# A recurrent attention block and an MLP in one kernel: loads of 48 rows instead of 128, four copies on another engine, and new orders of the work

## The chip, the cores and the metric

The kernel runs on one core of a Trainium2 chip. The metric is the device time of one execution in microseconds. The kernel before was run nine times: the median is 659.54 us, the lowest 658.38, the highest 661.29.

## The reference

For each of 4 batches and 8 heads, a state of 48 x 48 numbers is updated at each of 768 time steps and read out; the result goes through an MLP (384 to 2048 to 384) with a PReLU between. All of it is in float32.

```python
f = 1.0 / (1.0 + np.exp(-f_logit))
state = np.zeros((B, H, D, D))                 # B 4, H 8, D 48
for t in range(S):                             # S 768
    state = f[:, :, t, :, None] * state + np.einsum('bhd,bhe->bhde', k[:, :, t], v[:, :, t])
    y[:, :, t] = np.einsum('bhd,bhde->bhe', q[:, :, t], state)
x = y.transpose(0, 2, 1, 3).reshape(B * S, H * D)      # 3072 tokens of 384
h = x @ w_in                                   # 384 x 2048
g = np.maximum(h, 0.0) + alpha * np.minimum(h, 0.0)
out = g @ w_out                                # 2048 x 384
```

## The kernel before

**Steps.** Time is cut into 6 chunks of 128 and the batches into 2 pairs, so there are 12 steps (a chunk of a batch pair, 256 tokens); the chunk is the outer loop. Inside a chunk the recurrence is done without a loop over time: products of decays are formed for runs of 4 and blocks of 32 time steps, and matmuls build a matrix A of decayed products of q and k, which is then multiplied with v and, through the same matmuls, with the state carried from the half chunk before. The state lies in spare rows of the tile `vs`, beside v.

**Layout.** A head has 48 dimensions. Even heads lie in partitions 0 to 47, odd heads in 64 to 111 (`rows(par)`). The arrays `qT`, `kT`, `fT` in memory have 128 rows for each chunk, of which rows 48 to 63 and 112 to 127 are zeros put there by the host (`by_dim`). A load in `prepare` brings all 128 rows of a batch pair: 512 KB.

**Stages.** Each step has four Python generators. Each `next` on one of them emits one piece.

- `prepare` (6 pieces): loads of f, q, k and v; ScalarE takes the sigmoid of f (L250) and copies (L251, L253); VectorE multiplies decays into `qd` (L258 to L266). Then running sums of decays by VectorE, four copies into `us` by ScalarE (L275); the products `us` (L280, L289), `k4` (L295), `q3`, `ks`, `kh` (L307 to L328) on VectorE; last four copies of q3 into A by ScalarE (L340).
- `carry` (2 pieces): matmuls `off` (L356) with copies into A (L361) and transposes `pk` (L369) with copies into `ksn` (L372); then matmuls `pd` (L381) and `moved(0)`, which brings the state a half chunk on: VectorE multiplies the old state (L391) and adds the increment `pd` (L395). Where there is no state yet (chunk 0, first half) the increment is only copied (L397).
- `attend` (6 pieces): for each batch u of the pair, matmuls `raw` (L416) and `qu` (L431), whose results VectorE writes into `ad` under masks (L422, L436); two pieces of copies from ad into A by ScalarE (L445), one for each u; matmuls `py` (L456); then `moved(1)`, two copies of py into y (L465) and eight heads' DMAs that bring y in the layout `xT` (L472, half of them issued by ScalarE, half by SP).
- `network` (12 pieces): eight pieces, each of 6 matmuls `ph` (L486; two records each in the profile, 12 in all), a Relu by ScalarE (L491, `neg`) and two operations of VectorE that give `g` (L494); then matmuls `po` (L502) in four quarters, the last with the copies (L508) and the DMAs of the output.

**Weights.** `load_weights` gives two pairs of generators: `a` and `w` for w_in, `b` and `v` for w_out, 12 pieces each. An upper piece (`a`, `b`) is a DMA by SP (L163) and two operations of ScalarE (L168, L170). A rest piece (`w`, `v`) is three operations of VectorE (`lead` L176, `rest` L188, `power` L182: a triple) and a DMA of GpSimd that adds the leading parts to the tile (L191).

**Buffers.** PSUM tiles of the attention stages are `pair`s, of which there are two: raw, qu, raw, qu, off, pk, pd and py take turns. ph and po share four banks. The tiles f, q and k of a step come from the pool `work` with one buffer each.

**Order.** TensorE, VectorE and ScalarE execute exactly in the order in which the program emits; the queues of GpSimd and SP are ordered by a scheduler. The order comes from strings. In turn n, `P`, `O` and `S` stand for a piece of prepare, carry and attend of step n, `n` for a piece of the network of step n-1, `Q` for a piece of prepare of step n+1; a number repeats a key, and a key with nothing left is skipped. Turns 0 to 3 have their own strings (`first`), the other turns use `usual`. Turn n=2 so runs step 2's attention with step 1's network, and the fourth entry (n=3) step 3's attention with step 2's network.

```python
    def begin(n):
        ...
        return [stage(*steps[n], x) for stage in (prepare, carry, attend, network)]
...
            on = pieces | {"P": prep, "O": car, "S": att, "z": filling, "n": before, "Q": coming}
            for key in (first[n] if n < len(first) else usual).split():
                for _ in range(int(key[1:] or 1)):
                    if on[key[0]] is not None:
                        next(on[key[0]])
```

Of the kernel before, what the change touches and what calls it, by code (L numbers as in the profile page):

```python
# [8 lines left out]
F32 = mybir.dt.float32  # L9
# [12 lines left out]
U = 2  # L22
# [8 lines left out]
def kernel(  # L31
# [28 lines left out]
    nc = tc.nc  # L60
    B, NC, _, HP, _ = qT.shape
    DM = v.shape[-1]
    H = 2 * HP
# [5 lines left out]
    W = U * HP * C  # L69
# [12 lines left out]
    const = ctx.enter_context(tc.tile_pool(name="const", bufs=1))  # L82
    work = ctx.enter_context(tc.tile_pool(name="work", bufs=2))
# [3 lines left out]
    def pair(name):  # L87
        return psa.tile([128, 2, 512], F32, tag="pair", name=name)
# [35 lines left out]
    for m in range(1, NB):  # L124
        lo = UO[m] + (4 if m == 1 else 0)
        n = NB - m
# [4 lines left out]


    A = const.tile([128, U, H, C], F32, tag="A", name="A")
    nc.gpsimd.memset(A, 0.0)
    vs = []
    for bp in range(B // U):
# [75 lines left out]
    def rows(par):  # L212
        return slice(64 * par, 64 * par + D)

    def quads(t):
        return t.rearrange("p (n r) -> p n r", r=4)

    def halves(cc):

        return slice(CH * cc, CH * cc + CH), slice(CH * (1 - cc), CH * (1 - cc) + D)  # L220
# [8 lines left out]
    def prepare(bp, c, x):  # L229

        i = f"{bp}_{c}"
        b0 = U * bp
        loads = nc.gpsimd if bp or c else nc.sync

        def load(name, src, bufs=2):
            t = work.tile([128, W], F32, tag=name, name=f"{name}_{i}", bufs=bufs)
            loads.dma_start(out=t.rearrange("p (u x) -> p u x", u=U),  # L237
                              in_=src[b0:b0 + U, c].rearrange("u p h t -> p u (h t)"))
            return t

        f = quads(load("f", fT, 1))
        q = load("q", qT, 1)
        k = x["k"] = load("k", kT, 1)

        for cc in range(NC2):
            t_, _ = halves(cc)
# [25 lines left out]
        us = x["us"] = work.tile([128, G, UW], F32, tag="us", name=f"us_{i}", bufs=1)  # L272
# [21 lines left out]
        k4 = x["k4"] = work.tile([128, W], F32, tag="k4", name=f"k4_{i}", bufs=1)  # L294
# [43 lines left out]
        for cc in range(NC2):  # L338
            for par in range(2):
                nc.scalar.copy(A[halves(cc)[1], :, par * HP:(par + 1) * HP, CH * cc:CH * (cc + 1)],  # L340
                               q3[rows(par)].rearrange("p (u h c) s t -> p u h c (s t)", h=HP, c=NC2)[:, :, :, cc, 0:CH])
        yield

    def carry(bp, c, x):

        i = f"{bp}_{c}"
        q3, ks, kh, f64 = (x[n] for n in ("q3", "ks", "kh", "f64"))
        off = pair(f"off_{i}")
        for u in range(U):
            for hp in range(HP):  # L350
                for cc in range(NC2):
                    g = (u * HP + hp) * NC2 + cc
                    o = (u * HP + hp) * DB
                    for par in range(2):
                        r_ = rows(par)
                        nc.tensor.matmul(off[CH * cc:CH * cc + DB, par, o:o + DB],  # L356
                                         lhsT=kh[r_, g], rhs=q3[r_, g, 2], start=True, stop=True)
        for cc in range(NC2):
            s_ = slice(CH * cc, CH * cc + DB)
            for par in range(2):  # L360
                nc.scalar.copy(A[s_, :, par * HP:(par + 1) * HP, CH * cc + DB:CH * (cc + 1)],  # L361
                               off[s_, par, 0:U * HP * DB].rearrange("p (u h t) -> p u h t", u=U, h=HP))


        pk = pair(f"pk_{i}")
        for u in range(U):
            for hp in range(HP):
                a = (u * HP + hp) * NC2
                nc.tensor.transpose(pk[:, u, hp * 128:(hp + 1) * 128], ks[:, a:a + 2].rearrange("p c s t -> p (c s t)"), ident)  # L369
        ksn = work.tile([128, U, HP * 128], F32, tag="ksn", name=f"ksn_{i}", bufs=1)  # L370
        for u in range(U):
            nc.scalar.copy(ksn[:, u], pk[:, u])  # L372
        yield
        pd = pair(f"pd_{i}")
        for u in range(U):
            for hp in range(HP):
                for cc in range(NC2):
                    for par in range(2):
                        o = (u * HP + hp) * D
                        s_ = halves(cc)[0]  # L380
                        nc.tensor.matmul(pd[64 * par:64 * par + 64, cc, o:o + D],  # L381
                                         lhsT=ksn[s_, u, hp * 128 + 64 * par:hp * 128 + 64 * par + 64],
                                         rhs=vs[bp][s_, cc, u, (2 * hp + par) * D:(2 * hp + par + 1) * D], start=True, stop=True)

        def moved(cc):

            of, to = halves(cc)[1], halves(1 - cc)[1]
            was, then = (vs[bp][p, a, :, 0:DM].rearrange("p u (h e) -> p u h e", e=D)
                         for p, a in ((of, cc), (to, 1 - cc)))
            if c or cc:  # L390
                nc.vector.tensor_tensor(then, was, f64[of].unsqueeze(3).broadcast_to((D, U, H, D)), ALU.mult)  # L391
            for par in range(2):
                now = pd[rows(par), cc, 0:U * HP * D].rearrange("p (u h e) -> p u h e", u=U, e=D)
                if c or cc:
                    nc.vector.tensor_tensor(then[:, :, par:H:2], then[:, :, par:H:2], now, ALU.add)  # L395
                else:
                    nc.vector.tensor_copy(then[:, :, par:H:2], now)  # L397

        x["moved"] = moved
        moved(0)  # L400
        yield

    def attend(bp, c, x):

        i = f"{bp}_{c}"
        k, k4, us = (x[n] for n in ("k", "k4", "us"))


        for u in range(U):
            raw = pair(f"raw{u}_{i}")  # L410
            for hp in range(HP):
                for j in range(NJ):
                    g = (u * HP + hp) * NJ + j
                    for par in range(2):
                        r_ = rows(par)
# [4 lines left out]
            for d in range(4):  # L420
                n = 4 - d
# [4 lines left out]
            for hp in range(HP):  # L426
                for j in range(NJ):
                    g = (u * HP + hp) * NJ + j
                    for par in range(2):
                        r_ = rows(par)  # L430
                        nc.tensor.matmul(qu[DB * j:DB * (j + 1), par, hp * UW + 4:(hp + 1) * UW],  # L431
                                         lhsT=k4[r_, g * DB:(g + 1) * DB], rhs=us[r_, g, 4:UW], start=True, stop=True)
            for m in range(1, NB):
                lo = UO[m] + (4 if m == 1 else 0)
                n = DB - 4 * m
# [6 lines left out]
        for u in range(U):  # L442
            for j in range(NJ):
                s_ = slice(DB * j, DB * (j + 1))
                nc.scalar.copy(A[s_, u, :, s_], ad[s_, u].rearrange("p r h t -> p (r h) t"))  # L445
            yield
# [3 lines left out]
        for u in range(U):  # L450
            for hp in range(HP):
                for cc in range(NC2):
                    for par in range(2):
# [3 lines left out]
                                         lhsT=vs[bp][:, cc, u, hd * D:hd * D + 64],  # L457
                                         rhs=A[:, u, par * HP + hp, CH * cc:CH * (cc + 1)],
                                         start=True, stop=True)
# [7 lines left out]
        for hd in range(H):  # L467
            d = hd * D
            while d < (hd + 1) * D:
                n = min((hd + 1) * D, (d // 128 + 1) * 128) - d  # L470
                p0 = 64 * (hd % 2) + d - hd * D
                (nc.sync if hd % 2 else nc.scalar).dma_start(  # L472
                    out=xT[d % 128:d % 128 + n, d // 128].rearrange("p (u t) -> p u t", u=U),
                    in_=y[p0:p0 + n, :, hd // 2])
# [3 lines left out]
    def network(bp, c, x):  # L478
# [37 lines left out]

    steps = [(bp, c) for c in range(NC) for bp in range(B // U)]
    first = (
        "P2 a2 P2 w a2 w P O w P a w S2 O w Q S2 a w a S a S Q w2",
        "a P w a w a P w n P a n w b v w S b v n b n O v b v n b v S P S n b O b v n b S v2 n2 S n b v Q b v b n v b v2 Q3 S n Q",  # L520
        "n2 O n S n2 S Q S n S O n2 Q n Q2 n P S n S Q n Q",
        "n S n2 S Q n2 O n S n S Q n O Q2 n Q S2 Q n3",
    )
    usual = "O n2 S n2 S2 n O n Q n Q n S n2 S Q n S Q2 n Q"
    pieces = {key: part for keys, parts in (("aw", load_weights(w_in_sb, w_in, "w_in")),
                                            ("bv", load_weights(w_out_sb, w_out, "w_out")))
              for key, part in zip(keys, parts)}
# [1 line left out]
    def begin(n):  # L529
        if n >= len(steps):  # L530
            return [None] * 4
        x = {}
        return [stage(*steps[n], x) for stage in (prepare, carry, attend, network)]
# [68 lines left out]
```

## Time and profile before

The profiled execution took 659.54 us itself; its span, from the first to the last instruction, is 657.7 us. In the first 110 us the weights come in beside the first steps.

| what | value | from |
| --- | --- | --- |
| time, nine runs | 659.54 us median, 658.38 to 661.29 | times |
| profiled execution, span | 659.54 us, 657.7 us | profile |
| read from and written to HBM | 36.21 MB, 4.72 MB | page, part 3 |
| instructions of ph and po | 265.2 and 252.7 us of TensorE | page, part 5 |
| loads of f, q, k by GpSimd | 11 each, 512 KB, 4.3, 4.2, 4.5 us to landing | page, part 6 |
| loads of v by GpSimd | 22, 192 KB, 3.5 us to landing | page, part 6 |
| first off of step 0 | 18.45 us | timeline |
| first ph of steps 0 and 1 | 48.03 and 109.08 us | timeline |
| last weight DMA landed | 106.13 us | timeline |
| off of steps 4 and 5 | 210.2 and 260.6 us | timeline |

How to read it: an instruction that waits holds up all later ones of its engine. The list of waits gives, for each kind, how long the engine stood idle in total, how often, and the longest. A timeline row gives start, length and engine of a run of like instructions, and in brackets the idle time before it with what ended it. Granted clock 0.50 means that TensorE's matmuls take twice as long. A matmul in float32 shows as several instructions, so the counts are multiples of the calls in the code.

### The profile page before, as it was taken

The page shows a single profiled execution, that of the slowest core. Times are in us where ns is not written, and L with a number is a line of the kernel's source. Part 1 is how long each engine was busy: PE and PEld are TensorE (multiplying, and loading weights), DVE is VectorE, ACT ScalarE, POOL GpSimd, SP SyncE. Part 2 cuts the span into 40 slices and gives each one's busy share as a digit, 9 for nine tenths or more (in the row PEclk, how much of TensorE's full clock was granted, in tenths as well). Part 3 has the DMA queues.
Part 4 walks back from the last instruction along what each step waited for, and adds up shares of the span by engine and source line. Part 5 has one row for each costly group of instructions (what it writes and reads, how often), then busy time and mean ns, then how long its engine had stood idle before and what let it go on. Part 6 is the DMA issues. An engine that isn't in the chain of part 4 may idle for free.

```text
span 657.7 us, 17032 instructions
## 1 busy us (share of the span) xinstructions
PE 616.7 (94%) x7392; PEld 458.8 (70%) x7392; DVE 420.3 (64%) x897; ACT 266.8 (41%) x493; POOL 68.8 (10%) x109
## 2 busy tenths in 40 slices
PE   0547999999999999999999999999999999999997
PEld 0435866866876876876876876876876786786874
DVE  5999889693873685685585586486387486360220
ACT  5854892543443242451451550550460451430210
POOL 7222332000010000000000001001001000000000
PEclk9967999999999999999999999999999999999999
DMA  7979986122212113113113023023023011001000
GB/s 223 321 194 267 268 250 158 39 62 73 66 38 69 34 56 83 34 34 92 29 51 81 29 64 81 26 66 80 26 66 81 26 34 25 26 2 25 24 1 24
DMA packets 29129, 53.03 MB, mean 81 GB/s; under 512 B 4320, under 2 KB 16864, under 8 KB 29056
## 3 DMA queue, kind: packets, MB, share of 16 engines
q0 software_dynamic: 9616, 27.92, 15.8%
q1 hardware_dynamic: 13584, 21.63, 10.7%
q10 hardware_dynamic: 5856, 2.40, 1.7%
q8 instruction: 58, 0.95, 0.6%
q14 instruction: 15, 0.12, 0.1%
HBM read 36.21 MB, written 4.72 MB: 62 GB/s over the span
## 4 chain that ended last, share of the span: by engine, by line
PE 90%; DVE 5%; ACT 1%; POOL 1%; issue 1%; ACTq 1%; DVEq 0%; POOLq 0%
PE ph L486 38%; PE po L502 38%; PE py L456 3%; PE qu L431 3%; PE raw L416 3%; PE pd L381 2%; PE pk L369 2%; PE off L356 1%; DVE us L289 1%; DVE ad L436 1%; ACTq L472 1%; POOL vs L138 0%; DVE w_in_lead L176 0%; DVE us L280 0%; ACT w_in_pos L168 0%
## 5 line engine op out<-in xcount | busy, mean ns | idle before, releaser
L486 PE MATMUL ph<-xT,w_in_sb 128*128 128x256 f32 x1152 | 265.2, 387 | 8.8 <-DMA xT<-y 8.7
L502 PE MATMUL po<-w_out_sb,g 128*128 128x384 f32 x768 | 252.7, 488 | 0.0
L486 PEld LDWEIGHTS ph<-xT,w_in_sb 128*128 128x128 f32 x1152 | 218.3, 193 | 43.9 <-DMA w_in_sb<-w_in_lead 8.5
L502 PEld LDWEIGHTS po<-w_out_sb,g 128*128 128x128 f32 x768 | 144.8, 190 | 97.1 <-DMA w_out_sb<-w_out_lead 0.4
L494 DVE SCALAR_TENSOR_TENSOR g<-neg,om,ph 128x256 f32<-128x256 f32 x192 | 83.3, 477 | 151.8 <-ACT neg L491 151.6
L491 ACT ACTIVATE neg<-ph 128x512 f32<-128x512 f32 x96 | 57.7, 601 | 153.2 <-PE ph L486 125.0
L508 ACT COPY o<-po 128x384 f32<-128x384 f32 x24 | 11.5, 479 | 114.3 <-PE po L502 106.4
L436 DVE COPY_PREDICATED ad<-mquad,qu 128x224 f32<-128x224 int32 (+6 forms) x168 | 50.4, 300 | 8.4 <-DVE ad L422 0.5
L465 ACT COPY y<-py 128x512 f32<-128x512 f32 x24 | 12.9, 588 | 81.1 <-PE py L456 81.1
L289 DVE TENSOR_TENSOR us<-us,fs 128x768 f32<-128x768 f32 (+2 forms) x72 | 44.6, 620 | 0.3
L422 DVE COPY_PREDICATED ad<-mraw,raw 128x256 f32<-128x256 int32 (+1 forms) x96 | 42.4, 442 | 2.7
L445 ACT COPY A<-ad 32x256 f32<-32x256 f32 x96 | 38.4, 400 | 3.8 <-DVE ad L436 2.5
L391 DVE TENSOR_TENSOR vs<-vs,f 48x768 f32<-48x768 f32 x20 | 19.0, 952 | 30.4 <-PE py L456 30.0
L275 ACT COPY us<-qd 128x256 f32<-128x256 f32 x48 | 29.6, 664 | 12.2 <-DVE qd L258 7.6
L431 PE MATMUL qu<-us,k 48*32 48x112 f32 x1536 | 27.7, 276 | 5.1 <-DVE us L289 3.4
L258 DVE TENSOR_TENSOR qd<-qd,f 128x768 f32<-128x768 f32 (+2 forms) x36 | 27.4, 760 | 8.0 <-ACT qd L253 8.0
L340 ACT COPY A<-q 48x512 f32<-48x512 f32 x48 | 29.6, 617 | 6.2 <-DMA xT<-y 5.5
L237 POOL DMA_DIRECT2D k<-in_kT x11 | 8.4, 761 | 221.7 <-PE raw L416 196.7
L456 PEld LDWEIGHTS py<-A,vs 128*64 128x64 f32 x768 | 25.1, 145 | 7.2 <-issue 6.5
L456 PE MATMUL py<-A,vs 128*64 128x64 f32 x768 | 26.9, 231 | 0.9 <-DVE vs L397 0.5
L356 PE MATMUL off<-q,kh 48*32 48x32 f32 x768 | 9.4, 199 | 18.5 <-DVE q L307 18.5
L431 PEld LDWEIGHTS qu<-us,k 48*32 48x32 f32 x1536 | 22.1, 111 | 5.7 <-ACT w_out_pos L168 3.6
(64 smaller groups left out, 447.3 us busy)
## 6 DMA issues: line engine op xcount, KB each, us to landing
w_in_raw<-in_w_in SPq DMA_DIRECT2D x12, 511.8 KB, 5.6
w_out_raw<-in_w_out SPq DMA_DIRECT2D x12, 511.8 KB, 5.2
f<-in_fT POOLq DMA_DIRECT2D x11, 512.0 KB, 4.3
q<-in_qT POOLq DMA_DIRECT2D x11, 512.0 KB, 4.2
k<-in_kT POOLq DMA_DIRECT2D x11, 512.0 KB, 4.5
out<-o SPq DMA_DIRECT2D x24, 192.0 KB, 1.9
vs<-in_v POOLq DMA_DIRECT2D x22, 192.0 KB, 3.5
w_in_sb<-w_in_lead POOLq DMA_DIRECT2D x12, 256.0 KB, 5.7
```

Source lines behind the costliest of these rows:

```text
L275: nc.scalar.copy(q4[:, :, :, r], qdv[r][:, :, :, 0])
L289: nc.vector.tensor_tensor(us[:, :, UO[m]:UO[m] + 4 * n].rearrange("p g (i r) -> p g i r", r=4), us[:, :, skip:skip + 4 * n].rearrange("p g ...
L340: nc.scalar.copy(A[halves(cc)[1], :, par * HP:(par + 1) * HP, CH * cc:CH * (cc + 1)], q3[rows(par)].rearrange("p (u h c) s t -> p u h c (s ...
L422: nc.vector.copy_predicated(adu[:, :, :, d:4], mraw[:, d, :, d:4].bitcast(I32).unsqueeze(1).broadcast_to((128, H, NB, n)), rv[:, :, QO[d]: ...
L431: nc.tensor.matmul(qu[DB * j:DB * (j + 1), par, hp * UW + 4:(hp + 1) * UW], lhsT=k4[r_, g * DB:(g + 1) * DB], rhs=us[r_, g, 4:UW], start=T ...
L436: nc.vector.copy_predicated(ad[:, u, :, :, 4 * m:DB], mquad[:, lo:lo + n].bitcast(I32).unsqueeze(1).unsqueeze(1).broadcast_to((128, 2, HP, ...
L445: nc.scalar.copy(A[s_, u, :, s_], ad[s_, u].rearrange("p r h t -> p (r h) t"))
L456: nc.tensor.matmul(py[64 * par:64 * par + 64, u, o:o + CH], lhsT=vs[bp][:, cc, u, hd * D:hd * D + 64], rhs=A[:, u, par * HP + hp, CH * cc: ...
L486: nc.tensor.matmul(ph[:, j * T:(j + 1) * T], lhsT=w_in_sb[:, kt, (f + j) * 128:(f + j + 1) * 128], rhs=xT[:, kt], start=(kt == 0), stop=(k ...
L491: nc.scalar.activation(neg, phv, AF.Relu, scale=-1.0)
L494: nc.vector.scalar_tensor_tensor(g[:, j], neg[:, j], om[:, f + j:f + j + 1], phv[:, j], ALU.mult, ALU.add)
L502: nc.tensor.matmul(po[u][:, 0:DM], lhsT=gs[f // 2][:, f % 2, u * C:(u + 1) * C], rhs=w_out_sb[:, f], start=(f == 0), stop=(f == NF - 1))
```

## The change

Three parts. Line numbers below L133 stay; later ones shift by one, and by two after the loads.

1. The tiles f (now `ft`), q and k become three constant tiles. The first step still loads 128 rows by SP in one DMA per tensor. Every later step loads only the 48 rows of the even heads and the 48 rows of the odd heads, in two DMAs of 192 KB per tensor by GpSimd; the 32 other rows keep what they held. These rows of f go through the sigmoid again in every step; no matmul reads them.
2. The copy of the first increment of the state (L397, chunk 0, first half; two copies in each of steps 0 and 1) moves from VectorE to ScalarE.
3. All order strings are new: the four of the first turns and the usual one. The number of pieces of each kind is the same in all.

```diff
     A = const.tile([128, U, H, C], F32, tag="A", name="A")
+    ft, q, k = (const.tile([128, W], F32, tag=n, name=n) for n in ("ft", "q", "k"))
...
-        def load(name, src, bufs=2):
-            t = work.tile([128, W], F32, tag=name, name=f"{name}_{i}", bufs=bufs)
-            loads.dma_start(out=t.rearrange("p (u x) -> p u x", u=U),
-                              in_=src[b0:b0 + U, c].rearrange("u p h t -> p u (h t)"))
-            return t
-
-        f = quads(load("f", fT, 1))
-        q = load("q", qT, 1)
-        k = x["k"] = load("k", kT, 1)
+
+        def load(t, src):
+            for r_ in (rows(0), rows(1)) if bp or c else (slice(0, 128),):
+                loads.dma_start(out=t[r_].rearrange("p (u x) -> p u x", u=U),
+                                in_=src[b0:b0 + U, c, r_].rearrange("u p h t -> p u (h t)"))
+
+        load(ft, fT)
+        load(q, qT)
+        load(k, kT)
+        f = quads(ft)
...
-                    nc.vector.tensor_copy(then[:, :, par:H:2], now)
+                    nc.scalar.copy(then[:, :, par:H:2], now)
...
-        k, k4, us = (x[n] for n in ("k", "k4", "us"))
+        k4, us = x["k4"], x["us"]
...
     first = (
-        "P2 a2 P2 w a2 w P O w P a w S2 O w Q S2 a w a S a S Q w2",
-        "a P w a w a P w n P a n w b v w S b v n b n O v b v n b v S P S n b O b v n b S v2 n2 S n b v Q b v b n v b v2 Q3 S n Q",
-        "n2 O n S n2 S Q S n S O n2 Q n Q2 n P S n S Q n Q",
-        "n S n2 S Q n2 O n S n S Q n O Q2 n Q S2 Q n3",
+        "P3 a P w a P a w a w O S a w S2 a w Q O P S w Q S a2 S w2",
+        "a3 P2 w2 P w n a w n w S n b v b v n b v O b v n b S P S v b2 v n2 S v b v n O n S n b v Q b v b n b v3 Q S Q2 n Q",
+        "n2 O n S n2 S n2 S2 O n2 Q P n S n Q S Q n Q2",
+        "S n2 S n O n3 Q2 S n O Q n2 Q P Q S3 n3 Q",
     )
-    usual = "O n2 S n2 S2 n O n Q n Q n S n2 S Q n S Q2 n Q"
+    usual = "O n S n2 S Q n Q2 n S n O n S Q n2 Q S2 n Q n2"
```

## The prediction

> **What bounds the kernel now.** I read the page first, then the list of what TensorE waited for, then a table of stretches, then the timelines of TensorE, VectorE and ScalarE over the first 110 us.
>
> ```profile
> PE 616.7 (94%) x7392; PEld 458.8 (70%) x7392; DVE 420.3 (64%) x897; ACT 266.8 (41%) x493; POOL 68.8 (10%) x109
> ...
> PE   0547999999999999999999999999999999999997
> ...
> DVE  5999889693873685685585586486387486360220
> ...
> PEclk9967999999999999999999999999999999999999
> ```
>
> TensorE is busy 94% of 657.7 us, and its idle time lies in the first slices. VectorE is full there too. The list of waits (total, times, longest) has little else:
>
> ```profile
> PE off L356 <- DVE q L307: 18.5, 1, 18.5
> PE ph L486 <- DMA xT<-y: 8.7, 2, 8.4
> PE qu L431 <- DVE us L289: 3.4, 1, 3.4
> PE pk L369 <- DVE ks L325: 2.2, 1, 2.2
> ...
> PE pd L381 <- PE ph L486: 0.7, 1, 0.7
> ```
>
> All of these lie before 80 us. The table of stretches (length, then PE, PEld, DVE, ACT and POOL busy, clock, DMA share, GB/s) shows what a wait costs beside itself:
>
> ```profile
> 43.50:53.80 10.30, 5.46 (x12) 3.81 (x13) 9.61 (x18) 5.33 (x10) 3.32 (x4) 0.50 0.95 266
> 57.40:60.80 3.40, 0.04 (x3) 0.00 (x0) 3.39 (x10) 1.27 (x2) 0.85 (x1) 0.97 1.10 322
> 60.80:67.40 6.60, 6.54 (x76) 5.26 (x77) 6.37 (x16) 1.52 (x3) 1.71 (x2) 0.50 0.72 207
> 67.40:80.00 12.60, 11.90 (x248) 9.86 (x249) 10.80 (x29) 11.28 (x21) 4.17 (x5) 1.00 0.98 264
> 200.00:300.00 100.00, 100.00 (x1224) 74.34 (x1225) 61.35 (x131) 37.98 (x72) 5.56 (x8) 1.00 0.17 50
> ```
>
> From 200 to 300 us TensorE is never idle at clock 1.00: no transfer, copy or load can win anything there, and an order can only lose. The one dear wait is that at 57.4, for VectorE's last L289: 3.4 us with nothing to do, then 6.6 us at clock 0.50, worth 3.3 us more. TensorE's timeline shows it, and the smaller wait before pd:
>
> ```profile
> 60.86 1.75 PE L431 MATMUL qu<-us,k 48*32 48x112 f32 x64 [3.41 <-DVE us L289]
> 62.53 7.83 PE L486 MATMUL ph<-xT,w_in_sb 128*128 128x256 f32 x24
> ...
> 70.98 1.09 PE L369 MATMUL pk<-ident,ks 128*128 128x128 f32 x8
> ...
> 79.84 1.15 PE L381 MATMUL pd<-vs,ksn 64*64 64x48 f32 x64 [0.70 <-PE ph L486]
> ```
>
> And VectorE, otherwise without a gap from 25.6 to 60.7 us, stood still once, because the copies of L275 were behind five issues of xT in ScalarE's queue (41.75 to 46.26):
>
> ```profile
> 48.42 1.23 DVE L280 TENSOR_TENSOR us<-us,f 128x1024 f32<-128x1024 f32 x1 [0.68 <-ACT us L275]
> ```
>
> **The change part by part.** The profiled execution took 659.54 us, 657.7 of span and 1.84 around it; that is also the median of the nine runs (658.38 to 661.29). About 0.2%, or 1.3 us, is what can be told from no change.
>
> **Loads without the zero rows.** 33 loads of 512 KB become 66 of 192 KB (48 rows each), 128 KB less each time: 4.2 MB of the 36.21 MB read. At a DMA share of 0.17 (200 to 300 us) bytes are no limit. GpSimd issues 33 more, at 0.76 us (median of the k rows) 25 us of an engine that is 10% busy; only its own later DMAs queue behind them. The nearest row for the time to landing is that of v, two of 192 KB each: 3.5 us, against 4.5 for k in one piece. The second half is issued 0.76 later, so k is complete after 4.3 to 4.5 us, as before. In the usual order k is issued after raw of u=1 and read by L295 about 11 us later: that slack is the cover, and if it were gone the price would be the 1.0 us by which the two halves of v land apart. In the start stage 0.4 MB less (step 1) at the 266 GB/s of 43.5 to 53.8 us is 1.5 us of transfer, if transfers set the pace there. Bounds -1.5 to +1.0; I take 0, since VectorE and not a landing ended the waits above.
> The Trainium skill speaks against this part ("DMA: Bandwidth & Descriptors", section "Rules for kernel authors"): two transfers to disjoint halves of the partitions serialise, and one of 128 partitions is to be preferred. The trace agrees as far as the two halves of v land 1.0 us apart; with that on the path of 11 steps it would be +11 us, and with the slack above it is 0.
>
> **First increments on ScalarE.** Four copies (48x384), VectorE 0.56 us each, go. Two lie ahead of the wait at 57.4 (1.12 us), two among the weights of step 1. On ScalarE the nearest rows are 0.48 (L508, 128x384) and 0.59 (L465, 128x512); I take 0.55, so +1.1 in front of py of step 0, between sigmoid work and the copies of q3.
>
> **New orders, the start (gain).** Ahead of the last L289 VectorE now does one triple of a weight piece less (lead, rest, power: 1.13), one g pair less (0.79), the two copies less (1.12), and the idle 0.68 goes, since the L275 copies now precede y and the xT issues on ScalarE: 3.7 us, so L289 is done at 60.7 - 3.7 = 57.0. TensorE comes later instead. ScalarE, from VectorE's end with u=0 at 29.6 to 30.7, does A copies 1.65, one pos/neg pair 1.3, sigmoid 1.06, kr 0.6, qd 1.04, the two moved copies 1.1, four L340 2.5, A copies 1.65, L275 2.1, two pos/neg pairs 2.7, y 1.04: xT is issued at 46.3 to 47.4 instead of 41.75. Before, SP was held until 46.03 and the last piece landed 4.1 later, at 50.15; now that is 50.4 to 51.5. 24 passes of ph take 5.4 us at full and 10.9 at half clock; the clock stood at 0.50 until 53.8, so they end at 58 to 60, raw 0.9 later, and qu starts at 59 to 61 with its operand ready. The stall and the half-clock stretch lose their cause. Next late is pk, whose buffer VectorE frees with L436 of u=0: 57.0 plus 1.5 (L327, L307, L335), 2.3 (two triples), 1.7 (two g pairs), 0.6, L422 1.85, L436 2.32 gives 67.3, so pk at 67.4 against 70.98: 3.6 us. The 0.70 before pd goes (three ph pairs now cover it): 4.3. But then po arrives early for the last weights. Their last accumulation was issued at 100.7 and landed at 106.1; the last 1.33 of 16 rows of po (1.31 us each) started at 107.5. If that train stays where it is, only 1.4 of the 4.3 is kept; if it moves with VectorE, all. At 90.98 VectorE itself waited 1.55 us for a landing of this train, and the DMA share is 0.87 from 80 to 109.7, so I go nearer to the low end: a gain of 2.0.
>
> **New orders, the fourth entry (loss).** This is the turn that runs step 2's network with step 3's attention, once, at full clock, where TensorE never waited. First, off and pk now come after only three ph pairs, right behind qu of u=1. pk takes the buffer that qu leaves, once L436 has read it. From ph2's end VectorE's chain is neg 0.16+0.60, g 0.87, L422 1.87, L436 2.31: 5.8. TensorE gets there in raw 0.85, qu 0.84, ph4 2.69, off 0.69: 5.1. Wait 0.7. Second, the next step's first two prepare pieces stand before this step's A copies and after ph10. From ph10's end: neg 0.6, sigmoid 1.06, kr 0.56, qd 1.04, VectorE's five products 3.2, last L275 0.66, A copies of u=0 1.65, neg12 0.63, g12 0.88, L391 1.06, L395 1.11: 12.5. TensorE: ph12 2.69, pd 1.08, ph14 2.69, a quarter of po 5.16: 11.6. py waits 0.9. Third, ScalarE reaches the end of neg12 at 9.4 of this chain and still has neg14 0.6, four L340 2.5 and the A copies of u=1 1.65: 14.2. py's second half would start at 12.5 + 1.0 = 13.5 and waits 0.7. Sum 2.3; starts come up to 0.1 before the end of the instruction ahead, so a chain may be 0.3 shorter, or as much longer by hand-overs between engines: bounds 1.4 to 3.0. The other new entries (third and usual) I followed in the same way: the usual one has py's inputs 3.4 us early, and its step stays at the 50.33 us of the old one. I cost them at 0; a wait of 0.1 us each would be 0.8 over eight steps.
>
> **Sum.** 659.54 - 2.0 + 2.3 + 0 = 659.8. Own range 658.2 (gain 3.0, loss 1.7) to 660.9 (gain 1.4, loss 2.7).
>
> **Rivals.** *The gain stays and the loss is small.* The weight train moves with VectorE (4.3), the loss is at 1.4 to 2.3: 656.6 to 657.5, say 657.1. For it: the pieces are VectorE's work, which is 3.7 ahead. Against: landings were waited for at 90.98.
> *The clock stays down (the slower side).* ph starts some 3 us later, after a TensorE idle of 7 us or more, and a stretch half busy does not lift the clock: 5.46 us of 10.30 ran at 0.50 from 43.5 to 53.8. If it is not at 1.00 by 57 us, or drops at the wait before pk, one or two stretches of 3.4 us at half clock cost 1.7 to 3.4: 661.5 to 663.2, say 662.4. Against: without the stall at 57.4 there is dense work from 52 us on, and a wait of 0.70 at 79.1 left the clock at 1.00.
> The skill's rule ("TensorE: Matmul & The Clock Gate", "Part 1: The HAM clock gate") is a free-running window of about 3.4 us. By it a wait below 2 us costs only itself and this rival has no price (659.8); the row above, where a half-busy stretch stayed slow, speaks for 662.4.
> *Late halves.* If a split load were late in every step, 1.0 x 11: 670. ScalarE's sigmoid waited for f only 1.7 us in all, so there is room.
>
> **How the numbers follow.** The first case 0.50, small loss 0.18, clock 0.29, late halves 0.03. Faster than 658.2: 0.18 and a little of the first, 0.22. Slower than 660.9: 0.29 + 0.03 and 0.09 of the first, 0.41. Same: 0.37. The range 657.2 to 662.8 leaves out about a tenth at each end.
>
> **What would show it.** qu of step 1 without a wait and no 0.50 after 57.4; pk near 67.4; step 1's first ph near 107 instead of 109.1; three new waits in the fourth turn, at pk and twice at py, of 2.3 us; steps of 50.33 us after. Wrong if 0.50 shows after 60 us, if po waits over 3 us for weights, or if a step is longer than 50.4.

## The result, and the profile after

The changed kernel takes 662.46 us (median of 12 runs, 661.41 to 664.24) against 659.51 for the kernel before on the same chips (median of 38): 2.95 us more, a ratio of 1.0044 with a 95% interval of 1.0034 to 1.0054. The forecast was 659.8 within 657.2 to 662.8, with a chance of 0.41 for slower than 660.9, 0.37 for no change and 0.22 for faster. The time lies in the range, but the change is slower by more than can be mistaken for nothing. The profiled execution took 661.68 us, with a span of 659.9 against 657.7. The two profiled executions differ by 2.14 us and the medians by 2.95; the lines below account for the 2.14, and the rest of the 2.95 stays open.

The page of the changed kernel, busy time and tenths in 40 slices:

```profile
span 659.9 us, 17133 instructions
...
PE 616.0 (93%) x7392; PEld 457.5 (69%) x7392; DVE 416.0 (63%) x893; ACT 270.8 (41%) x497; POOL 83.7 (13%) x142
...
PE   0537999999999999999999999999999999999997
...
PEclk9867999999999999999999999999999999999999
...
HBM read 31.89 MB, written 4.72 MB: 55 GB/s over the span
```

TensorE has as much work as before and is idle longer. The 4.3 MB are no longer read, and no run here shows a gain from it. What TensorE waited for (total, times, longest; line numbers are two higher than before):

```profile
PE ph L488 <- DMA xT<-y: 11.6, 2, 9.0
PE py L458 <- ACT A L342: 2.5, 4, 2.0
...
PE pd L383 <- issue: 1.1, 1, 1.1
PE pk L371 <- DVE ks L327: 1.1, 1, 1.1
PE pk L371 <- DVE ad L438: 0.7, 1, 0.7
PE po L504 <- DMA w_out_sb<-w_out_lead: 0.7, 1, 0.7
PE py L458 <- DVE vs L397: 0.6, 1, 0.6
PE py L458 <- ACT A L447: 0.4, 1, 0.4
```

The wait of qu for L289 (3.4) is gone. In its place xT costs 11.6 instead of 8.7, py waits for ScalarE, and po for a weight. The lines "ad L438: 0.7", "vs L397: 0.6" and "A L447: 0.4" are the fourth entry, where TensorE's timeline has them in a part of the run that was dense before:

```profile
170.81 0.76 PE L358 MATMUL off<-q,kh 48*32 48x32 f32 x64
172.28 1.06 PE L371 MATMUL pk<-ident,ks 128*128 128x128 f32 x8 [0.72 <-DVE ad L438]
...
193.61 1.15 PE L458 MATMUL py<-A,vs 128*64 128x64 f32 x32 [0.60 <-DVE vs L397]
195.15 1.03 PE L458 MATMUL py<-A,vs 128*64 128x64 f32 x28 [0.40 <-ACT A L447]
...
211.79 0.76 PE L358 MATMUL off<-q,kh 48*32 48x32 f32 x64
```

Where the time came from is read from the same instruction in both traces:

| instruction starts at | before | after | difference |
| --- | --- | --- | --- |
| pk of step 1 | 70.98 | 69.59 | -1.39 |
| first po of step 0 | 86.20 | 84.36 | -1.84 |
| first ph of step 1 | 109.08 | 108.80 | -0.28 |
| off of step 2 | 114.66 | 114.13 | -0.53 |
| off of step 4 | 210.22 | 211.79 | +1.57 |
| off of step 5 | 260.55 | 262.57 | +2.02 |
| first ph of the last network | 612.75 | 614.99 | +2.24 |

The start was 1.84 us ahead when po began and gave nearly all of it back before po ended. The turns after off of step 2 then lost 2.10 us up to off of step 4 and 0.45 in the turn after it. Later steps take 50.33 again, but for 0.2 us in all.

### The profile page after: what moved, and what is told of

Its sections match the earlier page's. It is cut to its first block, busy times and chain, and to the rows that moved or that the text cites. A ratio compares the mean times of both kernels' runs of the same rounds, so it can differ in the third digit from the quotient of the medians.

```text
span 659.9 us, 17133 instructions
## 1 busy us (share of the span) xinstructions
PE 616.0 (93%) x7392; PEld 457.5 (69%) x7392; DVE 416.0 (63%) x893; ACT 270.8 (41%) x497; POOL 83.7 (13%) x142
## 4 chain that ended last, share of the span: by engine, by line
PE 81%; ACT 6%; DVE 6%; DMA 3%; issue 2%; ACTq 0%; POOL 0%; DVEq 0%; POOLq 0%
PE po L504 35%; PE ph L488 35%; PE py L458 3%; PE qu L433 2%; PE raw L418 2%; PE pd L383 1%; PE pk L371 1%; DVE ad L438 1%; DVE ad L424 1%; ACT A L342 1%; DMA xT<-y 1%; ACT A L447 1%; PE off L358 1%; DMA w_out_raw<-in_w_out 1%; DMA ft<-in_fT 1%
## 5 line engine op out<-in xcount | busy, mean ns | idle before, releaser
L488 PE MATMUL ph<-xT,w_in_sb 128*128 128x256 f32 x1152 | 262.8, 385 | 11.9 <-DMA xT<-y 11.6
L493 ACT ACTIVATE neg<-ph 128x512 f32<-128x512 f32 x96 | 57.4, 600 | 149.2 <-PE ph L488 125.3
L438 DVE COPY_PREDICATED ad<-mquad,qu 128x224 f32<-128x224 int32 (+6 forms) x168 | 50.3, 300 | 7.9
L239 POOL DMA_DIRECT2D k<-in_kT x22 | 12.8, 587 | 225.5 <-PE raw L418 225.5
L447 ACT COPY A<-ad 32x256 f32<-32x256 f32 x96 | 38.4, 400 | 5.7 <-DVE ad L438 4.4
L467 ACT COPY y<-py 128x512 f32<-128x512 f32 x24 | 12.9, 589 | 46.3 <-PE py L458 46.2
L458 PE MATMUL py<-A,vs 128*64 128x64 f32 x768 | 28.3, 232 | 3.5 <-ACT A L342 2.5
L260 DVE TENSOR_TENSOR qd<-qd,ft 128x768 f32<-128x768 f32 (+2 forms) x36 | 27.2, 754 | 3.7 <-ACT qd L255 3.7
L418 PEld LDWEIGHTS raw<-qd,k 48*32 48x32 f32 x1536 | 17.9, 107 | 9.7 <-issue 8.8
L358 PEld LDWEIGHTS off<-q,kh 48*32 48x32 f32 x768 | 8.0, 110 | 23.6 <-DVE q L309 18.3
```

The lines of the kernel that those rows point to most:

```text
L418: nc.tensor.matmul(raw[DB * j:DB * (j + 1), par, hp * C:hp * C + QW], lhsT=k[r_, g * DB:(g + 1) * DB], rhs=qd[r_, g], start=True, stop=True)
L438: nc.vector.copy_predicated(ad[:, u, :, :, 4 * m:DB], mquad[:, lo:lo + n].bitcast(I32).unsqueeze(1).unsqueeze(1).broadcast_to((128, 2, HP, ...
L458: nc.tensor.matmul(py[64 * par:64 * par + 64, u, o:o + CH], lhsT=vs[bp][:, cc, u, hd * D:hd * D + 64], rhs=A[:, u, par * HP + hp, CH * cc: ...
L488: nc.tensor.matmul(ph[:, j * T:(j + 1) * T], lhsT=w_in_sb[:, kt, (f + j) * 128:(f + j + 1) * 128], rhs=xT[:, kt], start=(kt == 0), stop=(k ...
L493: nc.scalar.activation(neg, phv, AF.Relu, scale=-1.0)
```

## The experiments

Each kernel was timed beside the kernel before on the same chip.

| run | time, us | before there | ratio, 95% interval |
| --- | --- | --- | --- |
| new orders alone | 661.92 | 659.67 | 1.0031 (1.0017 to 1.0044) |
| changed, old third and fourth entries | 659.32 | 659.67 | 0.9999 (0.9986 to 1.0011) |
| changed, old first two entries | 669.27 | 659.67 | 1.0141 (1.0119 to 1.0164) |
| old orders, new loads and copies | 666.12 | 659.67 | 1.0102 (1.0082 to 1.0122) |
| new loads alone | 660.62 | 659.51 | 1.0016 (1.0006 to 1.0026) |
| new copies alone | 665.12 | 659.51 | 1.0083 (1.0070 to 1.0096) |
| changed, no accumulation of w_out | 660.03 | 659.51 | 1.0007 (0.9999 to 1.0016) |
| before, no accumulation of w_out | 658.23 | 659.51 | 0.9987 (0.9979 to 0.9996) |
| before, new third and fourth entries | 661.65 | 659.85 | 1.0026 (1.0016 to 1.0036) |
| changed, old fourth entry | 659.66 | 659.85 | 1.0000 (0.9991 to 1.0008) |
| changed, old third and fourth entries, old loads | 659.79 | 659.85 | 1.0001 (0.9991 to 1.0011) |
| changed, old third and fourth entries, xT early | 664.50 | 659.85 | 1.0070 (1.0055 to 1.0085) |

**New orders alone.** The kernel before with all five new strings.

> The new orders with the old loads and the old copies on VectorE. Theory A (the orders cost it: three waits in the fourth entry, 1.7 us, some 0.4 in the step after it, and a start that gives back nothing because xT lands at 54.6): as the changed kernel or slower by the 1.1 us of VectorE's two copies at most, 662.2 to 663.6, with the waits at pk and py of the fourth entry in place. Theory B (the split loads of 192 KB crowd the DMA queues in the start stage and make xT late): 659.5 to 660.7, xT landed before 53.

661.92 is some 0.3 below the first theory's span and well above the second's. The new orders cost 2.2 of the 2.95 us by themselves, without the new loads and copies.

**Old third and fourth entries.** In the changed kernel:

```diff
-        "n2 O n S n2 S n2 S2 O n2 Q P n S n Q S Q n Q2",
-        "S n2 S n O n3 Q2 S n O Q n2 Q P Q S3 n3 Q",
+        "n2 O n S n2 S Q S n S O n2 Q n Q2 n P S n S Q n Q",
+        "n S n2 S Q n2 O n S n S Q n O Q2 n Q S2 Q n3",
```

> The changed kernel with the third and fourth entries of the old orders. Theory A: the waits at pk and py near 172 to 195 go, and the 0.45 us in the next step with them: 2.2 us less than the changed kernel, 660.0 to 660.5. If only the waits themselves count (1.7): 660.7. Theory B: these waits are hidden elsewhere, no more than 0.5 less, 662.0.

659.32: 3.1 us less than the changed kernel, a little beyond the first theory, and no different from the kernel before. So the loss lies in these two entries, and the new start and the new usual entry, with the new loads and copies, are worth nothing that can be measured either way.

**Old first two entries**, the rest as changed:

> The changed kernel with the first two entries of the old orders. Theory A: the start is worth nothing either way (0.28 us in the two profiles), 661.7 to 662.8. Theory C (the new start loses in the median what the one profile does not show, 0.7 us): 661.2 to 661.8. If the new start gains the 2.0 us of the prediction: 664.5.

669.27, outside all three expectations: 6.8 us slower than the changed kernel. The next run has the same cost, and the two after it find it.

**Old orders with the new loads and copies:**

> The old orders with the new loads and with the first increments copied by ScalarE. Theory A: 658.4 to 659.6 (two copies of 0.56 us less ahead of the wait at 57.4, nothing from the loads). Theory B (split loads crowd the queues): 661 or more, with xT landing after 52.

666.12, which neither theory had. ScalarE stood 8.95 us before the moved copies, waiting for pd, which pointed to the copies. Each part was then put alone on the kernel before:

```diff
-                    nc.vector.tensor_copy(then[:, :, par:H:2], now)
+                    nc.scalar.copy(then[:, :, par:H:2], now)
```

> The kernel before with the first increments copied by ScalarE alone. If the copies are the cost: 665 to 667, ScalarE idle for 8 to 9 us before its first copy, with the sigmoid of the next step and the A copies queued behind it, py near 41.6 instead of 35.2. If it is the loads: 658.4 to 660.

665.12, 5.6 us. ScalarE's timeline with the copies alone:

```profile
27.81 0.78 ACT L170 ACTIVATE w_in_neg<-w_in_raw,bias 128x512 int16<-128x512 uint16 x1
34.80 0.96 ACT L397 COPY vs<-pd 48x384 f32<-48x384 f32 x2 [6.22 <-PE pd L381]
35.67 1.05 ACT L250 ACTIVATE f<-f 128x1024 f32<-128x1024 f32 x1
```

In the old order the increment is emitted before the sigmoid of the next step. On VectorE that place was free; on ScalarE the two copies wait 6.22 us for pd, and the sigmoid, the A copies that py needs and y stand behind them (py began at 39.11 instead of 35.16, and step 1's first ph at 114.61 instead of 109.08). In the changed kernel the sigmoid and the copies L253 and L255 stand ahead of them, and there they start without a wait:

```profile
33.84 1.04 ACT L255 COPY qd<-q 128x1024 f32<-128x1024 f32 x1
34.79 0.95 ACT L399 COPY vs<-pd 48x384 f32<-48x384 f32 x2
35.77 2.54 ACT L342 COPY A<-q 48x512 f32<-48x512 f32 x4
```

So the new start is needed to bear the copies, and the two parts can't be judged one at a time.

> The kernel before with the new loads alone. If the copies on ScalarE are what cost 6.5 us under the old orders (ScalarE stood 8.95 us before L399, for pd): 659.0 to 660.2, no change. If it is the loads of 48 rows: 664 to 666.

660.62: neither "no change" nor the 5 us, but about 1.1 us more (0.4 to 1.7 by the interval). In its profile TensorE waits 3.04 us in the middle of a group of raw, until 32.1 us, for nothing that the profile shows, and step 1's first ph comes 2.0 us later than in the kernel before (111.11). The same place waits 2.04 and 2.48 us in the two other runs with the new loads under the old start, but also 1.91 in one of the four profiles with the old loads there (the late entries alone), so the loads can't be shown to cause it.

**The accumulations of w_out left out**, in the changed kernel and in the one before:

```diff
-            nc.gpsimd.dma_start(out=flat[:, n:n + WP], in_=got.pop(n)[1], accum_op=ALU.add)
+            t = got.pop(n)[1]
+            if dst is w_in_sb:
+                nc.gpsimd.dma_start(out=flat[:, n:n + WP], in_=t, accum_op=ALU.add)
```

> The changed kernel without the 12 DMAs that add the leading parts to w_out (that part of the weights is left out of the output). If the train of weights holds po and with it the end of the first network (po waited at 100.1 and through TensorE's weight loads): step 1's first ph at 106.0 to 107.5 instead of 108.8, 660.3 to 661.3. If not: 662.0 to 662.8 and ph at 108.4 or later.

> The kernel before without the same 12 DMAs. Theory of the train: po never waited for it there, so 659.0 to 659.7 and ph at 108.6 to 109.2. If the DMAs cost time in another way (their traffic, VectorE waiting for their landing at 90.98): 658.0 to 658.8.

The changed kernel gains 2.43 us (662.46 to 660.03) and the one before 1.28 (659.51 to 658.23). The first is a little better than expected. The second lies where the other theory put it, 658.0 to 658.8, but the profiles don't show that the DMAs cause it: 1.22 of the 1.25 us by which step 1's first ph is earlier there (107.83 against 109.08) are present at pk, at 69.76, before the first of these DMAs was issued in the kernel before (70.99). In the changed kernel step 1's first ph came at 106.91, as the train's theory had it, and the last 48 records of po, which had gaps, ran through. TensorE, changed kernel:

```profile
84.36 5.78 PE L504 MATMUL po<-w_out_sb,g 128*128 128x384 f32 x16
90.06 2.08 PE L458 MATMUL py<-A,vs 128*64 128x64 f32 x64
92.08 8.01 PE L504 MATMUL po<-w_out_sb,g 128*128 128x384 f32 x24
100.80 8.17 PE L504 MATMUL po<-w_out_sb,g 128*128 128x384 f32 x24 [0.71 <-DMA w_out_sb<-w_out_lead]
```

And without the accumulations:

```profile
91.32 15.75 PE L506 MATMUL po<-w_out_sb,g 128*128 128x384 f32 x48
106.91 5.34 PE L490 MATMUL ph<-xT,w_in_sb 128*128 128x256 f32 x24
```

The last 48 records of po take 15.6 us from start to start of what follows (91.32 to 106.91, and 93.47 to 109.08 before); in the changed kernel 16.7. The first 16 take 5.70 instead of 5.26 before. These 1.1 and 0.44 are what the start gave back. Only the 1.1 is for the weights: among the first 16, TensorE's weight loads stood 0.70 us for ScalarE's `neg`, and without the accumulations these 16 take even longer, 6.12 (83.19 to 89.31), since po waits for g. Changed kernel, weight loads (PEld):

```profile
85.35 4.17 PEld L504 LDWEIGHTS po<-w_out_sb,g 128*128 128x128 f32 x14 [0.70 <-ACT neg L493]
...
100.79 4.81 PEld L504 LDWEIGHTS po<-w_out_sb,g 128*128 128x128 f32 x16 [1.32 <-DMA w_out_sb<-w_out_lead]
```

**The new third and fourth entries on the kernel before:**

> The kernel before with the new third and fourth entries alone (old loads, copies, start and usual entry). If the waits of the fourth entry are the whole loss, whatever runs before and after: waits at pk 0.7, py 0.6 and 0.4 as in the changed kernel, and 1.7 to 2.5 more than before, 661.2 to 662.0; with all that undoing them gave (3.1): 662.6. If they cost only behind the new start: 659.5 to 660.3.

661.65, 1.8 us more, with the same waits:

```profile
173.41 1.07 PE L369 MATMUL pk<-ident,ks 128*128 128x128 f32 x8 [0.72 <-DVE ad L436]
...
194.75 1.15 PE L456 MATMUL py<-A,vs 128*64 128x64 f32 x32 [0.62 <-DVE vs L395]
196.30 1.03 PE L456 MATMUL py<-A,vs 128*64 128x64 f32 x28 [0.40 <-ACT A L445]
```

Here the step after takes 50.32 us (off at 212.95 and 263.27), not 50.78: with the old usual entry behind it the fourth costs nothing further.

**The old fourth entry alone in the changed kernel**, with one more Q at the end of the third, which keeps the count:

> The changed kernel with the old fourth entry alone; the third stays new but for one more Q at its end. If the loss is in the fourth entry: as with both undone, 659.0 to 660.0. If the third has a share: 660.3 to 661.5.

659.66, against 662.46: 2.8 us, and not to be told from the kernel before. The new third entry costs nothing that can be measured; the fourth is the whole loss.

**Two tries for a faster kernel**, both from the run with the old third and fourth entries: the old loads, and y with the xT DMAs ahead of the last two upper pieces of the first turn ("S2 a2 w2" for "S a2 S w2").

> Copies on ScalarE, new first, second and usual entries, old third and fourth, and the old loads of 128 rows. If the split loads cost about 1 us also under the new start, as alone: 658.0 to 658.6, faster than both kernels. If the new start hides them: 659.0 to 659.7.

659.79: behind the new start the split loads make no difference that can be measured, so their 1.1 us does not add to the rest. po shows the train of weights most plainly here:

```profile
101.05 9.70 PE L502 MATMUL po<-w_out_sb,g 128*128 128x384 f32 x24 [2.12 <-DMA w_out_sb<-w_out_lead]
```

> As the run with the old third and fourth entries (659.32), but y and xT are emitted before the last two upper pieces of the first turn. If the late xT sets the start: xT issued 2.7 us earlier, the 24 passes of ph done near 57 to 58, and 658.0 to 658.8. If the train of weights sets it: 659.0 to 659.9, or 0.5 to 1.5 more, since the upper pieces are now later.

664.50, 4.6 us slower than the kernel before, worse than the expected 0.5 to 1.5. xT was issued at 43.44, 2.3 us earlier than in the changed kernel, and ph's first 24 rows ended at 57.4. But the upper pieces then stood behind the xT issues in ScalarE's queue, and VectorE, which works through the weights, stood 6.44 us. VectorE and TensorE:

```profile
50.44 0.43 DVE L177 TENSOR_TENSOR w_in_lead<-w_in_pos,w_in_neg 128x512 bf16<-128x512 bf16 x1 [6.44 <-ACT w_in_neg L171]
```

```profile
63.19 1.75 PE L433 MATMUL qu<-us,k 48*32 48x112 f32 x64 [4.89 <-DVE us L291]
```

So this run shows the price of the upper pieces behind the issues; what an earlier xT alone would give, it doesn't show. No run here beats the kernel before by more than its interval, with all of its work done.

## Why the prediction was right or wrong

**The gain at the start, 2.0 us: wrong in size; it was 0.28 in the profile, and nothing in the medians** (659.32 against 659.67 with the old late entries). The first links held: qu has no wait for L289, whose last ended at 56.42 where 57.0 was worked out; the 0.70 before pd went. (VectorE's idle time before was not only the 0.68: it also stood 0.27 and 0.15 us near 30.5 and 32.7.) Then two sizes failed. First, xT: "now that is 50.4 to 51.5". Its issues began at 45.74, a little earlier than the 46.3 worked out, but its last piece let ph go on at 54.65. I took the 4.1 us that the DMAs needed after SP was free; they were issued by 50.0 and took 3.3 to 6.3 us each to land, with the DMA share at 0.99. So ph ran at half clock to 59 us, and pk came at 69.59, not 67.4. The stretches in the changed kernel (columns as in the prediction):

```profile
43.50:53.80 10.30, 1.19 (x2) 0.50 (x2) 10.27 (x18) 4.88 (x8) 3.55 (x5) 0.60 0.99 205
53.80:57.40 3.60, 2.75 (x7) 2.24 (x8) 3.60 (x10) 1.41 (x2) 2.00 (x2) 0.50 1.01 382
57.40:60.80 3.40, 3.40 (x13) 2.86 (x12) 2.48 (x8) 1.51 (x3) 0.85 (x1) 0.73 1.12 328
60.80:67.40 6.60, 6.60 (x152) 5.58 (x151) 5.83 (x15) 1.92 (x4) 1.70 (x2) 1.00 1.00 273
```

Second, the slack at the last weights. The lead at po was 1.84 instead of 4.3, and 0.28 of it was left at step 1's first ph. The prediction's "If that train stays where it is, only 1.4 of the 4.3 is kept" had the right mechanism: the train did stay, with its last accumulation issued at 100.71 and landed at 106.01, against 100.65 and 106.13 before. But the 1.4 was mis-sized. It lets the last piece be needed at 107.5, for the last 1.33 of the 16 weight tiles. The piece of 512 columns holds the whole last tile (384 columns) and the last third of the tile before, and that tile's matmuls wait for all of it: two tiles, 8 records of po. In the kernel before these began at 106.50, so the slack was 0.37:

```profile
106.50 2.74 PE L502 MATMUL po<-w_out_sb,g 128*128 128x384 f32 x8
```

With the old third and fourth entries the same 8 records show the wait:

```profile
105.73 2.82 PE L504 MATMUL po<-w_out_sb,g 128*128 128x384 f32 x8 [0.32 <-DMA w_out_sb<-w_out_lead]
```

| run | last weights landed | last 8 records of po | first ph of step 1 |
| --- | --- | --- | --- |
| before | 106.13 | 106.50 | 109.08 |
| changed | 106.01 | 106.15 | 108.80 |
| new orders alone | 105.71 | 105.75 | 108.44 |
| changed, old third and fourth entries | 105.59 | 105.73 | 108.38 |
| changed, old fourth entry | 106.39 | 106.52 | 109.18 |

In these four runs with the new start the 8 records begin 0.04 to 0.14 us after the landing, whatever the lead was before. Leaving out the accumulations lets the changed kernel gain about 1.15 us more than the one before, which fits; that the kernel before gains too is not explained.

**The fourth entry, 2.3 us: right in place and mechanism, each wait close.** pk 0.72 for 0.7, py 0.60 for 0.9 and 0.40 for 0.7. Listed waits come to 1.72, the turns from off of step 2 to off of step 4 to 2.10. The rest lies at the same places: from the start of off to that of pk 1.47 us instead of 0.69, from py to the next po 3.45 instead of 2.02. Undone, it gives 2.8 (the fourth alone) to 3.1 (with the third); put alone on the kernel before, 1.8.

**The usual entry at 0: 0.45 too little.** In the step after the fourth entry qu waits 0.18 us for a copy of ksn, and that step is 50.78. The run with the old usual entry behind the late entries has 50.32 there, and the new usual entry behind the old fourth 50.33 (off at 209.94 and 260.27), so it is the pair of new entries that costs it. A step longer than 50.4 was one of the prediction's own signs of being wrong. The other usual steps were costed rightly, but for 0.2 us in all.

**The loads at 0:** right behind the new orders; alone they cost 1.1, near the bound of +1.0, and the cause stays open. The Trainium skill's advice against two transfers to disjoint halves ("DMA: Bandwidth & Descriptors", "Rules for kernel authors") agrees with the sign of the one and finds no support in the other. **The copies:** their price in the changed kernel was right (0.95 for both, without a wait), but the prediction did not see that the same edit costs 5.6 us in the old order.

**The rivals.** The time is that of the second rival (662.4), and its condition was met, the clock not at 1.00 by 57 us: it came back about 4.6 us after ph went on at 54.65, worked out from 22 records in 7.26 us. But the half-clock stretch is not what made the change slower. With the old fourth entry it is there too (22 records in 7.15 us), and the time is that of the kernel before. Nor would its absence have saved the gain: with the new orders alone off of step 1 came 2.1 us earlier than in the changed kernel (66.83 against 68.91), but 1.29 us went at pk, for VectorE's L436, 1.09 at py, for the copy L397 on VectorE, and po then stood for the weights all the same, so that step 1's first ph was only 0.36 earlier. What made the change slower is the fourth entry, which stood in my likeliest case, without the gain that was to pay for it. That the total came so near to the second rival's is luck: its price was for a half-clock stretch. The gain of the first rival did not come, and split loads were never late in a steady step. The waits of 0.4 to 0.7 us in the fourth turn left the clock at 1.00 (granted clock from 163 to 213 us of the changed kernel); here the trace agrees with the Trainium skill's rule of a window of about 3.4 us ("TensorE: Matmul & The Clock Gate", "Part 1: The HAM clock gate").

## What to carry to other kernels

Where one engine is without a gap in the steady state, an order of a single turn can be costed by hand to some tenths: follow each chain from a fixed event to the waiting instruction, and set it against what the busy engine has to do meanwhile. A gain in a stage fed by transfers is worth only the slack to the next train of transfers; find that slack first, at the first instruction that reads any part of the last piece (here 0.37 us, where 1.4 was expected), and treat it as the ceiling unless the train moves too. An edit that moves an instruction to another in-order engine has the price of everything queued behind it there, so it must be judged together with the order.

## What the runs showed that was not expected

A stretch that was 2.75 of 3.60 us busy still ran at clock 0.50 (53.80 to 57.40 of the changed kernel). TensorE waited without a cause in the profile near 28 to 35 us in many runs, 1.1 us before pd in those with the new start and 1.9 to 3.0 in raw in some with the old one; that stays open. In the four profiles with the old start where raw stopped (1.91 to 3.04 us), it stopped after 21 of its 64 records, and a 16 KB transfer on the DMA queue that the page calls "instruction" ended 1.2 to 1.4 us before raw went on; a late fetch of instructions is a candidate that no run tests. Issuing the five xT DMAs kept ScalarE's queue for 4.3 to 5.5 us.
